# Columns by DMA transpose for half of the norm rows, a later mask fill, and a new matmul order in an attention loop

## The chip, the cores and the metric

The kernel runs on one core of one Trainium2 chip. The metric is the time of one execution on the device in microseconds (us). All numbers come from timed runs, or from profiled executions of the same kernels. The profiled span (first to last instruction) is some 1.5 to 2 us shorter than the timed execution. Engines: PE = TensorE matmul, DVE = VectorE, ACT = ScalarE, POOL = GpSimd, SP = SyncE; a "q" behind a name is that engine's instruction queue, where DMAs are issued.

A run counts as slow when it is over 1.5% above the fastest of its kernel; ratios use fast runs alone.

## The reference, cut to what matters

```python
x  = A_x                                    # 2048 rows of 512, bf16
xn = layernorm(x)
# A: attention with 32 heads of 16; row s sees rows s, s-2, ..., s-14
q, k, v = split(xn @ wqkv)
s  = softmax_over_8(q . k) . v @ wo
# B: mixer and MLP
h  = gelu(layernorm(xn) @ w1)               # then rows shifted by +-1 and +-2, @ w2
x1 = xn + shifted(h) @ w2
B  = x1 + gelu(layernorm(x1) @ w3) @ w4
out = x + s * silu(B)
```

Row s sees only rows of its own parity, so the kernel splits the rows by parity: p = 0 (chunks 0 and 1, 512 rows each) and p = 1 (chunks 2 and 3). "Second parity" means chunks 2 and 3. The attention is done in 18 units, nine per parity, of about 120 queries. It adds mask values to the scores by extra rows in the operands kT (keys) and qT (queries). Those rows are made once, written to a small memory buffer `mask_d`, and spread from there into kT and qT by DMA ("mask fill").

## The kernel before

Rows must become columns (features on partitions) before a matmul. The kernel before does that on PE: 16 transposes per chunk, a copy out by DVE, and for the second layernorm (a factor r2 per row) one more matmul that spreads r2 and a multiplication.

```python
def transposes(c, h):                        # half a chunk
    for j in range(2):
        for dt in range(ND):
            nc.tensor.transpose(pt[:, dt, j, :], x_c[:, 2*h + j, dt*P:(dt+1)*P], ident)
    nc.vector.tensor_copy(out=xnT[p][:, :, ...], in_=pt)
# rr_spread: diag(r2) by DVE -> one 128x512 matmul -> ACT copy; rr_mult: xn2T = xnT * that
...
for c in range(1, NCH):
    if c + 1 < NCH: ln_stats(c + 1)
    stage_tr(c)                              # PE transposes of chunk c
    stage_w1(c - 1)                          # first layer of B
    rr_spread(c); rr_mult(c)
    if c + 1 < NCH:
        ln_norm(c + 1); stage_qk(c)          # queries and keys
    if c == 2: fill_mask(0, 0); fill_mask(0, 1)
    if c == 1: build_mask()
stage_b(0)                                   # w2, x1, its norm; columns by DMA transpose
stage_w1(3); stage_b(1); stage_qk(3); stage_b(2)
stage_w3(0); stage_b(3); stage_w3(1); stage_w3(2); stage_w3(3)
...
# attention loop, unit n; w4 matmuls (and wo matmuls from n = 10) are spread in as filling
prs = [scores(p, u, 0)]
for f in fill[n][0]: f()                     # 8 of 11 w4 matmuls of a tile (n < 10)
prs.append(scores(p, u, 1))
for f in fill[n][1]: f()                     # the other 3
if prev is not None: weighted(*prev)         # prob @ values of the unit before, and its copy out
va = values(next unit)
```

(`...` marks cuts.) `stage_b` already has the pattern that the change uses more widely: write normed rows to memory with a plain DMA, read them back with a DMA transpose, both on the sync queue.

The softmax here doesn't subtract the row's maximum and nothing guards it: scores larger than these inputs give would overflow.

## Time and profile before

| | before |
|---|---|
| time, median of the four runs of the first comparison | 213.30 us (212.88 to 213.85) |
| profiled span | 211.9 us |
| PE busy | 201.7 us |
| granted TensorE clock | 0.999 |

From the page of the kernel before: busy us of each engine (share of the span) and number of instructions; then, below the cut, the shares of the chain of waits that ended last.

```profile
PE 201.7 (95%) x1978; PEld 96.5 (46%) x2007; DVE 131.0 (62%) x254; ACT 139.6 (66%) x160; POOL 55.5 (26%) x118
...
PE 80%; DVE 7%; DMA 5%; ACT 2%; issue 2%; POOL 1%; SPq 1%; DVEq 0%; ACTq 0%
```

PE is busy nearly always, and the chain runs over PE.

The timeline of PE, before, in the stretch that the change rebuilds. Columns: start, length, engine, source line, operation, output and inputs, shapes, count.

```profile
28.35 1.06 PE L321 MATMUL tr_ps<-ident,xn_96 128*128 128x128 bf16 x16
29.24 3.62 PE L391 MATMUL w_ps<-xn2T,w_sb 128*128 128x512 bf16 x15
32.70 0.39 PE L348 MATMUL rrep_ps<-xn2T,ones_bf 128*128 128x512 bf16 x1
32.93 7.07 PE L372 MATMUL qk_ps<-xnT_150,wqk_sb 128*128 128x512 bf16 x32
39.83 1.06 PE L321 MATMUL tr_ps<-ident,xn_96 128*128 128x128 bf16 x16
40.73 3.62 PE L391 MATMUL w_ps<-xn2T,w_sb 128*128 128x512 bf16 x15
44.18 0.38 PE L348 MATMUL rrep_ps<-xn2T,ones_bf 128*128 128x512 bf16 x1
```

No idle time stands in brackets behind any line: PE goes from one stage to the next. The transposes of a chunk (start 28.35 to next start 29.24) cost 0.89 us, the spreading matmul 0.23.

The timeline of the sync queue, before: the existing round trip through memory in `stage_b`.

```profile
55.02 0.40 SPq L436 DMA_DIRECT2D x1n_dram<-xn_662  x1
57.97 2.09 SPq L441 DMA_TRANSPOSE x1nT<-x1n_dram  x1
```

A write of 512 KB lets its transpose issue 2.95 us later. The issue of the transpose takes 2.1 us.

One unit of the attention loop, before, from the chain in order of time (start, length, what). `s_ps` are scores, `w_ps` w4, `o_ps` weighted values, `v_ps` values of the next unit.

```profile
132.45 0.34 PE s_ps L537 x16
132.79 1.83 PE w_ps L480 x8
134.63 0.51 PE s_ps L537 x16
135.14 0.76 PE w_ps L480 x3
135.89 0.53 PE o_ps L565 x32
136.43 0.32 PE v_ps L516
...
137.40 0.34 PE s_ps L537 x16
```

A unit takes 137.40 - 132.45 = 4.95 us. Sixteen full matmuls of 512 columns take 3.45 us (40.73 to 44.18 above; one record is missing there), 0.216 us each, so eight of them are 1.73 us, and the group takes 1.83.

### The profile page before, as it was taken

The page shows a single profiled execution, that of the slowest core. Times are in us where ns is not written, and L with a number is a line of the kernel's source. Part 1 is how long each engine was busy: PE and PEld are TensorE (multiplying, and loading weights), DVE is VectorE, ACT ScalarE, POOL GpSimd, SP SyncE. Part 2 cuts the span into 40 slices and gives each one's busy share as a digit, 9 for nine tenths or more (in the row PEclk, how much of TensorE's full clock was granted, in tenths as well). Part 3 has the DMA queues.
Part 4 walks back from the last instruction along what each step waited for, and adds up shares of the span by engine and source line. Part 5 has one row for each costly group of instructions (what it writes and reads, how often), then busy time and mean ns, then how long its engine had stood idle before and what let it go on. Part 6 is the DMA issues. An engine that isn't in the chain of part 4 may idle for free.

```text
span 211.9 us, 4839 instructions
## 1 busy us (share of the span) xinstructions
PE 201.7 (95%) x1978; PEld 96.5 (46%) x2007; DVE 131.0 (62%) x254; ACT 139.6 (66%) x160; POOL 55.5 (26%) x118
## 2 busy tenths in 40 slices
PE   8998999999999999999989999999999999998991
PEld 2544454544444444444444444444445544454440
DVE  6879396338839456000014666767767889688785
ACT  2098797943393625565599888788597888975310
POOL 4645774001120202000000008508039070253000
PEclk9999999999999999999999999999999999999999
DMA  5999314998240275599930003724325542445142
GB/s 152 375 395 389 117 8 6 147 145 108 99 99 3 99 198 99 140 174 126 120 39 3 0 3 61 216 80 76 114 82 141 168 103 33 129 121 107 31 147 99
DMA packets 30990, 25.16 MB, mean 119 GB/s; under 512 B 15960, under 2 KB 26424, under 8 KB 30968
## 3 DMA queue, kind: packets, MB, share of 16 engines
q1 hardware_dynamic: 27224, 19.02, 40.0%
q0 software_dynamic: 2192, 4.57, 9.1%
q10 hardware_dynamic: 1552, 1.27, 2.0%
q8 instruction: 16, 0.26, 0.6%
q14 instruction: 6, 0.05, 0.1%
HBM read 16.15 MB, written 4.37 MB: 97 GB/s over the span
## 4 chain that ended last, share of the span: by engine, by line
PE 80%; DVE 7%; DMA 5%; ACT 2%; issue 2%; POOL 1%; SPq 1%; DVEq 0%; ACTq 0%
PE w_ps L458 18%; PE w_ps L480 16%; PE qk_ps L372 10%; PE v_ps L516 7%; PE s_ps L537 7%; PE w_ps L421 6%; PE wo_ps L677 6%; PE w_ps L391 5%; PE o_ps L565 4%; DMA xn_95<-in_A_x_dram 3%; DMA oT_2427<-orw 2%; ACT prob L544 2%; DVE l1s_243 L284 1%; DVE l1s_299 L284 1%; DVE sg L686 1%
## 5 line engine op out<-in xcount | busy, mean ns | idle before, releaser
L544 ACT ACTIVATE prob<-s_ps 128x960 bf16<-128x960 f32 (+2 forms) x72 | 62.7, 925 | 11.6 <-PE s_ps L537 11.2
L480 PE MATMUL w_ps<-w_sb,h3T 128*128 128x512 bf16 (+1 forms) x174 | 43.6, 381 | 0.2 <-issue 0.2
L458 PE MATMUL w_ps<-x1nT,w_sb 128*128 128x512 bf16 (+1 forms) x173 | 38.2, 379 | 0.2
L464 ACT ACTIVATE h3T<-w_ps 128x1024 bf16<-128x1024 f32 x20 | 20.5, 1024 | 20.9 <-PE w_ps L458 20.9
L599 POOL DMA_DIRECT2D oT_1480<-orw x24 | 12.4, 525 | 61.3 <-DVE orw L572 61.3
L458 PEld LDWEIGHTS <-w_sb 128*128 128x128 bf16 (+1 forms) x176 | 17.6, 100 | 20.4
L480 PEld LDWEIGHTS <-h3T 128*128 128x128 bf16 (+1 forms) x176 | 14.7, 98 | 16.4
L521 DVE CAST v_aug_145<-v_ps 128x512 bf16<-128x512 f32 (+1 forms) x9 | 6.1, 681 | 23.1 <-PE v_ps L516 23.0
L572 DVE CAST orw<-o_ps 128x960 bf16<-128x960 f32 (+2 forms) x18 | 19.7, 1097 | 0.4 <-PE o_ps L565 0.4
L372 PEld LDWEIGHTS <-wqk_sb 128*128 128x128 bf16 x136 | 13.3, 98 | 14.3 <-issue 0.3
L599 POOL DMA_DIRECT2D oT_2427<-orw x20 | 10.1, 513 | 20.9 <-DVE orw L572 20.9
L487 DVE TENSOR_TENSOR xn_95<-w_ps,xn_95 128x512 bf16<-128x512 f32 x8 | 5.5, 692 | 16.0 <-PE w_ps L480 16.0
L372 PE MATMUL qk_ps<-xnT_149,wqk_sb 128*128 128x512 bf16 (+1 forms) x71 | 14.3, 355 | 0.3 <-DVE xnT_149 L324 0.2
L391 PE MATMUL w_ps<-xn2T,w_sb 128*128 128x512 bf16 x61 | 14.3, 379 | 0.2
L372 PE MATMUL qk_ps<-xnT_150,wqk_sb 128*128 128x512 bf16 x64 | 14.1, 379 | 0.0
L262 POOL TENSOR_SCALAR l3r<-l3m 128x4 f32<-128x4 f32 x4 | 1.0, 246 | 43.4 <-DVE l3m L270 43.4
L380 ACT ACTIVATE qT_155<-qk_ps 128x1024 bf16<-128x1024 f32 x4 | 4.1, 1030 | 9.8 <-PE qk_ps L372 9.8
L427 DVE TENSOR_TENSOR xn_96<-w_ps,xn_96 128x1024 bf16<-128x1024 f32 x4 | 4.9, 1216 | 8.3 <-PE w_ps L421 8.3
L421 PE MATMUL w_ps<-w_sb,hT_160 128*128 128x512 bf16 x32 | 9.5, 379 | 0.0
L516 PE MATMUL v_ps<-wv_sb,xnT_150 128*128 128x512 bf16 (+1 forms) x28 | 8.9, 383 | 0.4
L391 PEld LDWEIGHTS <-w_sb 128*128 128x128 bf16 x64 | 6.1, 98 | 6.8
L421 PE MATMUL w_ps<-w_sb,hT_159 128*128 128x512 bf16 x30 | 9.1, 379 | 0.1
(161 smaller groups left out, 328.8 us busy)
## 6 DMA issues: line engine op xcount, KB each, us to landing
w_sb<-in_B_w_dram SPq DMA_DIRECT2D x1, 1376.0 KB
w_sb<-in_B_w_dram SPq DMA_DIRECT2D x1, 1280.0 KB
wqk_sb<-in_A_wqkv_dram SPq DMA_DIRECT2D x2, 512.0 KB
w_sb<-in_B_w_dram SPq DMA_DIRECT2D x2, 512.0 KB
xn_96<-in_A_x_dram SPq DMA_DIRECT2D x4, 256.0 KB
xo_1598<-in_A_x_dram POOLq DMA_DIRECT2D x4, 256.0 KB, 3.9
xo_2228<-in_A_x_dram POOLq DMA_DIRECT2D x4, 256.0 KB, 3.7
out_dram<-xo_1598 SPq DMA_DIRECT2D x3, 256.0 KB
```

The costliest lines, as they stand in the source:

```text
L372: nc.tensor.matmul(pt[:, b, h : h + n], lhsT=wqk_sb[:, dt, nt * P : (nt + 1) * P], rhs=xnT[p][:, dt, k * CH + h : k * CH + h + n], start=( ...
L391: nc.tensor.matmul(pt[:, b, :], lhsT=w1_sb[:, dt, g * P : (g + 1) * P], rhs=xn2T[:, dt, :], start=(dt == 0), stop=(dt == ND - 1),)
L421: nc.tensor.matmul(pt[:, j, :], lhsT=w2_src(p, g, m0), rhs=w2_sb[:, g, :], start=(g == 0), stop=(g == ND - 1),)
L458: nc.tensor.matmul(pt[:fs, ft % 2, :], lhsT=w3_sb[:, dt, ft * P : ft * P + fs], rhs=x1nT[:, dt, :], start=(dt == 0), stop=(dt == ND - 1),)
L464: last["gelu"] = nc.scalar.activation(h3T[:, 2 * a : 2 * a + 2, :], pt, AF.Gelu_apprx_tanh)
L480: nc.tensor.matmul(pt, lhsT=h3[c][:fs, ft, jj * P : (jj + 1) * P], rhs=w4_sb[:fs, ft, :], start=(ft == 0), stop=(ft == NF - 1),)
L516: nc.tensor.matmul(vp[:nk, :], lhsT=xnT[p][:, dt, k0 : k0 + nk], rhs=wv_sb[:, dt, :], start=(dt == 0), stop=(dt == ND - 1),)
L537: nc.tensor.matmul(st[:nk, b, i * nq : (i + 1) * nq], lhsT=kT[p][e][r : r + 32, dt, k0 : k0 + nk], rhs=qT[p][e][r : r + 32, dt, q0 : q0 + ...
L544: nc.scalar.activation(prv[:nk, 2 * h : 2 * h + 2], st[:nk, :, 0 : 4 * nq], AF.Exp, scale=SCALE)
L572: pin(nc.vector.tensor_copy(out=orw[p][:, :, :, q0 - ra : q0 - ra + nq], in_=op[:, :, 0 : 4 * nq].rearrange("p j (s q) -> p j s q", q=nq),))
L599: (nc.scalar if (p, r) == (1, 2) and jj else nc.gpsimd).dma_start(out=oT[p][DH * hh : DH * (hh + 1), :, ra : ra + rw], in_=orw[p][32 * cg ...
L677: nc.tensor.matmul(pt, lhsT=oT[p][:, dt, i * P : (i + 1) * P], rhs=wo["sb"][:, dt, lo:hi], start=(dt == 0), stop=(dt == ND - 1),)
```

## The change

Its intent, in three parts:

1. Chunks 2 and 3 get their columns from memory: two writes and two DMA transposes per chunk. wv and w4 are loaded at about 60 us instead of at the start, so that these writes and transposes come ahead of all later loads.
2. The mask rows of the queries are filled behind the DMA transposes of the feed-forward stage. The mask buffer is now written by POOL, and the mask built on POOL behind chunk 2's r2.
3. In the attention loop the weighted values stand directly behind the second scores. Their copy out stays behind the filling; exponentials and tanh are pinned in order; units 10 to 13 split the w4 matmuls differently.

The diff, cut to its core:

```diff
-    wv_sb / w4_sb loads on nc.sync at the start
+    late_loads(): the same loads on nc.gpsimd, issued after last["r3"]
...
         for w in range(2):
-            pin(nc.sync.dma_start(out=mask_d[w].rearrange("r (g l) -> g r l", l=W), in_=rows[w]))
+            pin(nc.gpsimd.dma_start(out=mask_d[w].rearrange("r (g l) -> g r l", l=W), in_=rows[w]))
...
+    def dma_tr(c):
+        pin(nc.sync.dma_start(out=xn_dram[0, cs, :]..., in_=x_c))
+        for j in range(TPC):                      # xn2 = x_c * r2, four DVE operations
+            pin(nc.vector.tensor_scalar(out=xn2[:, j, :], in0=x_c[:, j, :], scalar1=r2[:, j : j + 1], ...))
+        pin(nc.sync.dma_start(out=xn_dram[1, cs, :]..., in_=xn2))
+        pin(nc.sync.dma_start_transpose(out=xnT[p][:, :, cs], in_=xn_dram[0, cs, :]))
+        pin(nc.sync.dma_start_transpose(out=xn2Ts[c], in_=xn_dram[1, cs, :]))
...
-    for c in range(1, NCH): ...
+    ln_stats(2)
+    stage_tr(1)
+    stage_w1(0)
+    rr_spread(1)
+    ln_norm(2)
+    dma_tr(2)
+    with tc.issue_after(last["r2"].ins):
+        build_mask()
+    rr_mult(1)
+    stage_qk(1)
+    ln_stats(3)
+    ln_norm(3)
+    dma_tr(3)
+    stage_w1(1)
+    stage_qk(2)
+    fill_mask(0, 0)
+    stage_w1(2)
     stage_b(0)
     stage_w1(3)
     stage_b(1)
+    with tc.issue_after(last["r3"].ins):
+        late_loads()
     stage_qk(3)
     stage_b(2)
     stage_w3(0)
     stage_b(3)
+    fill_mask(0, 1)
...
-            t, a, b, c = (n // 2 + 5, 0, 4, 5) if n % 2 == 0 else (n // 2 + 5, 5, 9, NF)
+            t, a, b, c = (n // 2 + 5, 0, 5, 5) if n % 2 == 0 else (n // 2 + 5, 5, NF, NF)
...
         prs.append(scores(p, u, 1))
+        if prev is not None:
+            op = weighted(*prev)
         for f in fill[n][1]:
             f()
         if prev is not None:
-            weighted(*prev)
+            keep(*prev[0:2], op)                  # the copy out
```

More of the change, by code (lines that the diff above doesn't have):

```diff
@@ L80 @@
     x1n_dram = dram.tile([S, D], BF16, name="x1n_dram")
+    xn_dram = dram.tile([2, M, D], BF16, name="xn_dram")
     def bigt(shape, name):
@@ L148 @@
     nc.sync.dma_start(out=w3_sb, in_=B_w3.rearrange("(dt q) f -> q dt f", q=P))
-    wv_sb = const.tile([P, ND, D], BF16, name="wv_sb")
-    nc.sync.dma_start(out=wv_sb, in_=wqkv_v[:, :, 2 * D : 3 * D])
-    w4_sb = midt([P, NF, D], "w4_sb")
-    nc.sync.dma_start(
-        out=w4_sb[:, 0 : NF - 1, :],
-        in_=B_w4[0 : (NF - 1) * P, :].rearrange("(ft q) n -> q ft n", q=P),
-    )
-    nc.sync.dma_start(out=w4_sb[0:FL, NF - 1, :], in_=B_w4[(NF - 1) * P : F, :])
     nc.scalar.preload_act_table_set("gelu_apprx_tanh_and_others")
@@ L187, in build_mask @@
         gp = nc.gpsimd
-        tab = sm4.tile([P, 3, P + 24], BF16, name="m_tab", tag="s4")
+        tab = fin.tile([P, 3, P + 24], BF16, name="m_tab", tag="f")
         for i, o, v in ((0, 0, -7), (0, 15, 8), (1, 1, -7), (1, 16, 7)):
@@ L243, in fill_mask, with late_loads @@
                 )
+    late = {}
+    def late_loads():
+        late["wv"] = const.tile([P, ND, D], BF16, name="wv_sb")
+        pin(nc.gpsimd.dma_start(out=late["wv"], in_=wqkv_v[:, :, 2 * D : 3 * D]))
+        late["w4"] = midt([P, NF, D], "w4_sb")
+        pin(
+            nc.gpsimd.dma_start(
+                out=late["w4"][:, 0 : NF - 1, :],
+                in_=B_w4[0 : (NF - 1) * P, :].rearrange("(ft q) n -> q ft n", q=P),
+            )
+        )
+        pin(nc.gpsimd.dma_start(out=late["w4"][0:FL, NF - 1, :], in_=B_w4[(NF - 1) * P : F, :]))
     NV = 2
@@ L262, in rsqrt_eps @@
         nc.gpsimd.tensor_scalar(out=dst, in0=var, scalar1=EPS, scalar2=None, op0=ALU.add)
-        nc.gpsimd.tensor_tensor(out=dst, in0=dst, in1=nhalf[:, 0 : dst.shape[-1]], op=ALU.pow)
+        return nc.gpsimd.tensor_tensor(out=dst, in0=dst, in1=nhalf[:, 0 : dst.shape[-1]], op=ALU.pow)
     def layer_stats(src, name):
@@ L271, in layer_stats @@
         rstd = small.tile([P, TPC], F32, name=name + "r", tag=name + "r")
-        rsqrt_eps(rstd, mv[:, :, 1])
+        last["r3"] = rsqrt_eps(rstd, mv[:, :, 1])
         return mv, rstd
@@ L277 @@
     lns = {}
+    last = {}
     def ln_stats(c, j0=0, n=TPC):
@@ L308, in ln_norm @@
         if j0 + n == TPC:
-            rsqrt_eps(r2, r2)
+            last["r2"] = rsqrt_eps(r2, r2)
     xn2Ts = {}
@@ L331, in stage_tr @@
             transposes(c, h)
+    def dma_tr(c):
+        p, k = c // 2, c % 2
+        cs = slice(k * CH, (k + 1) * CH)
+        x_c = xn[p][:, k * TPC : (k + 1) * TPC, :]
+        pin(nc.sync.dma_start(out=xn_dram[0, cs, :].rearrange("(i q) d -> q i d", q=P), in_=x_c))
+        r2 = r2s.pop(c)
+        xn2 = sm4.tile([P, TPC, D], BF16, name="xn2", tag="s4")
+        for j in range(TPC):
+            pin(
+                nc.vector.tensor_scalar(
+                    out=xn2[:, j, :], in0=x_c[:, j, :], scalar1=r2[:, j : j + 1], scalar2=None, op0=ALU.mult
+                )
+            )
+        pin(nc.sync.dma_start(out=xn_dram[1, cs, :].rearrange("(i q) d -> q i d", q=P), in_=xn2))
+        pin(nc.sync.dma_start_transpose(out=xnT[p][:, :, cs], in_=xn_dram[0, cs, :]))
+        xn2Ts[c] = sm4.tile([P, ND, CH], BF16, name="xn2T", tag="s4")
+        pin(nc.sync.dma_start_transpose(out=xn2Ts[c], in_=xn_dram[1, cs, :]))
     def rr_spread(c):
@@ L444 @@
     h3 = {}
-    last = {}
     def stage_w3(c):
@@ L480, in half @@
                     nc.tensor.matmul(
-                        pt, lhsT=h3[c][:fs, ft, jj * P : (jj + 1) * P], rhs=w4_sb[:fs, ft, :],
+                        pt, lhsT=h3[c][:fs, ft, jj * P : (jj + 1) * P], rhs=late["w4"][:fs, ft, :],
                         start=(ft == 0), stop=(ft == NF - 1),
@@ L491, in half @@
                     st["sig"] = fin.tile([P, D], BF16, name="sig", tag="f")
-                    nc.scalar.activation(st["sig"], x_i, AF.Tanh, scale=0.5)
+                    pin(nc.scalar.activation(st["sig"], x_i, AF.Tanh, scale=0.5))
         def gate():
@@ L516, in values @@
                 nc.tensor.matmul(
-                    vp[:nk, :], lhsT=xnT[p][:, dt, k0 : k0 + nk], rhs=wv_sb[:, dt, :],
+                    vp[:nk, :], lhsT=xnT[p][:, dt, k0 : k0 + nk], rhs=late["wv"][:, dt, :],
                     start=(dt == 0), stop=(dt == ND - 1),
@@ L543, in scores @@
             with tc.issue_after(last["gelu"].ins):
-                nc.scalar.activation(
+                pin(nc.scalar.activation(
                     prv[:nk, 2 * h : 2 * h + 2], st[:nk, :, 0 : 4 * nq], AF.Exp, scale=SCALE
-                )
+                ))
         return pr
@@ L551, in weighted @@
         r = next(i for i, x in enumerate(runs[p]) if u < x[1])
-        ra = runs[p][r][2]
         if u == runs[p][r][0]:
@@ L571, in weighted, with keep @@
                     )
+        return op
+    def keep(p, u, op):
+        q0, nq, k0, nk = units[u]
+        r = next(i for i, x in enumerate(runs[p]) if u < x[1])
+        ra = runs[p][r][2]
         pin(nc.vector.tensor_copy(
@@ L716 @@
     stage_qk(0, [1, 2, 3])
-    for c in range(1, NCH):
-        if c + 1 < NCH:
-            ln_stats(c + 1)
-        stage_tr(c)
-        stage_w1(c - 1)
-        rr_spread(c)
-        rr_mult(c)
-        if c + 1 < NCH:
-            ln_norm(c + 1)
-            stage_qk(c)
-        if c == 2:
-            fill_mask(0, 0)
-            fill_mask(0, 1)
-        if c == 1:
-            build_mask()
+    ln_stats(2)
[15 more added lines that the diff above has]
+    stage_w1(2)
     stage_b(0)
@@ L758 @@
         fill[n][0].append(lambda t=t, a=a, b=b: w4s[t][0](a, b))
+        if b == NF and n < 14:
+            fill[n + 1][0].append(w4s[t][1])
         if c > b:
@@ L803 @@
     )
-    weighted(*prev, tag="s")
+    keep(*prev[0:2], weighted(*prev, tag="s"))
     final_tile(1, 0, tag="b")
```

## The prediction

> **What bounds it now.** TensorE. The profile's busy table has PE at 201.7 of 211.9 us; the stretch table shows 9.9 to 10.0 us in nearly every 10 us from 30 to 110, and 9.84 to 9.89 from 120 to 180. The chain of waits is 80% PE. PE's idle time is about 10 us: the start (1.05 us, then warm-up), 0.67 us at 21 us (weights waiting for the diagonal from DVE), 0.52 us at the first exponentials, and the tail after 188 us. The granted clock is 0.999. So only PE time removed, or tail waits removed, can show.
>
> **What the change does.**
> 1. Chunks 2 and 3 lose their PE transposes (0.89 us of chain each: 16 matmuls) and the matmul that spreads r2 (0.22 us each): 2 x 1.11 = 2.2 us of PE, all on the chain. DVE loses two copies (1.25 us a chunk) and one multiplication (1.23), and gains four scalings (1.38); ACT loses a 0.6 us copy. None of those bound.
> 2. Added instead, per chunk: two 512 KB writes and two DMA transposes on the sync queue. The existing round trip of x1n shows the cost: write issued 55.02, transpose issued 57.97, its issue 2.1 us, data moving to about 62: some 7 us; with a second transpose about 9. My schedule: chunk 2's norm is written from about 22.5 us (the order of the DVE timeline), its transposes issue at 25.4 and 27.5, columns land at about 29.6 to 31.7. PE wants them for queries and keys at about 31.8 (two 3.45/6.9 us stages after 21.4) and the scaled ones at 38.7. The margin is 0 to 2 us. Chunk 3 must land by about 45.6; I get 42 to 45, the later if the two mask writes (2048 pieces of 16 bytes each), now issued by POOL, delay its rstd.
> 3. The DMA engines were full until 22.9 us (7.3 MB of loads). Moving wv and w4 (1.9 MB) to about 60 us frees them at about 18 us, so the new writes meet an idle queue. The moved loads fill idle DMA time.
> 4. Mask rows for queries go to about 88 us; they need about 7 us (before: 16 transfers in 40 to 52 us at 145 GB/s) and are wanted at 104. Free.
> 5. Attention loop: weighted values directly behind scores. The Trainium skill, "TensorEngine Tiling (Array Packing)", Key Properties, says that changing tiling mode drains TensorE. The trace agrees: eight w4 matmuls between two score groups take 1.83 us, against 8 x 0.216, so a return to tiles costs about 0.1 us; after the score group the cost is the same whatever follows. One such switch goes in 13 of 18 units: 1.3 us. Now that exponentials and tanh are pinned in order, tanh may come 0.05 to 0.1 us ahead of a ready exponential, and the score groups already wait some 0.15 us for exponentials: I count 0.9 us.
>
> Sum: 2.2 + 0.9 = 3.1 us, less an expected 0.3 us of new waits.
>
> **Predicted: 210.8 us, 208.6 to 214.0. Faster by over 2%: 0.18; within 2%: 0.74; slower: 0.08.**
>
> **What would show it.** No PE idle before the queries-and-keys matmuls of chunk 2 (else step 2 fails); the feed-forward stage starts about 2.2 us sooner than 65.1; the loop's period falls from 4.94 to about 4.87 us; the tail after the last scores is unchanged at about 22 us.
>
> **What would make it wrong.** DVE waiting for POOL's mask table ahead of the scaling, so that chunk 2's transposes come late and PE idles 1 to 4 us; POOL writing descriptors for the masks so long that chunk 3 stalls its first-layer matmuls; the late loads slowing x1n's second transpose, which landed only about 1 us ahead of its use; ACT, not PE, setting the loop's period.

## The result, and the profile after

The changed kernel took 218.32 us (median of four runs, 218.03 to 218.90) against 213.30. A ratio here is the mean time of one kernel's fast runs over that of the other's of the same rounds, so not quite the ratio of the medians: 1.0237, 95% interval 1.0202 to 1.0273. It is slower, and outside my range.

The same lines of the page, after:

```profile
PE 199.6 (92%) x1944; PEld 95.2 (44%) x1973; DVE 127.3 (59%) x248; ACT 138.3 (64%) x158; POOL 60.3 (28%) x123
...
PE 55%; DMA 15%; POOL 7%; DVE 7%; ACT 7%; SPq 4%; issue 3%; DVEq 0%; ACTq 0%
```

PE's busy time did fall, by 2.1 us (by 3.9, to 197.8, in a1 below, where no matmul runs at half clock), but the chain has left PE for DMA, POOL and the sync queue. The timeline of PE, after, shows where:

```profile
29.08 3.62 PE L419 MATMUL w_ps<-xn2T,w_sb 128*128 128x512 bf16 x15
32.53 7.07 PE L400 MATMUL qk_ps<-xnT,wqk_sb 128*128 128x512 bf16 x32
39.44 3.62 PE L419 MATMUL w_ps<-xn2T,w_sb 128*128 128x512 bf16 x15
42.89 3.62 PE L449 MATMUL w_ps<-w_sb,hT 128*128 128x512 bf16 x16
50.79 5.93 PE L419 MATMUL w_ps<-xn2T,w_sb 128*128 128x512 bf16 x16 [4.28 <-DMA xn2T<-xn_dram]
56.55 3.62 PE L449 MATMUL w_ps<-w_sb,hT 128*128 128x512 bf16 x16
```

The transposes and spreading matmuls of chunks 2 and 3 are gone, and chunk 2's columns came in time (no idle before 32.53). But chunk 3's first layer (50.79) waited 4.28 us for its scaled columns, and then took 50.79 to 56.55 = 5.76 us where the same stage takes 3.45 elsewhere. Stretches of the same trace, after (length, then busy us of PE, weight load, DVE, ACT and POOL, then granted clock, DMA share and GB/s; the DMA share adds up the times of packets and can pass 1), say why:

```profile
48.00:49.00 1.00, 0.00 (x0) 0.00 (x0) 1.00 (x2) 0.00 (x0) 0.00 (x0) 0.83 1.22 204
50.00:51.00 1.00, 0.21 (x1) 0.13 (x2) 0.03 (x1) 0.00 (x0) 0.80 (x2) 0.50 1.22 145
55.00:56.00 1.00, 1.00 (x5) 0.45 (x4) 0.00 (x0) 0.44 (x1) 0.00 (x0) 0.76 1.04 105
```

The granted clock fell to half during the idle time, and stayed there until 55 to 56 us. The Trainium skill, "TensorE: Matmul & The Clock Gate", What's actually happening, describes this: an idle window halves the clock until PE has been busy for a window again. The trace agrees as to the half clock and the return, which came about 5 us after the restart; the fall came only about 2 us after the last matmul (46.5 to between 48 and 49), sooner than the idle window of that page (last section).

What held chunk 3 back is read from the timelines of POOL and of the sync queue, after. First POOL:

```profile
31.23 2.58 POOL L226 DMA_DIRECT2D mask_d<-m_rows  x2
33.89 0.24 POOL L270 TENSOR_SCALAR l1r<-l1m 128x4 f32<-128x4 f32 x1
```

Then the sync queue:

```profile
36.70 0.37 SPq L347 DMA_DIRECT2D xn_dram<-xn  x1
38.45 0.37 SPq L356 DMA_DIRECT2D xn_dram<-xn  x1
42.56 3.22 SPq L357 DMA_TRANSPOSE xnT<-xn_dram  x1
45.95 2.03 SPq L359 DMA_TRANSPOSE xn2T<-xn_dram  x1
```

POOL computes chunk 3's 1/sigma (`l1r`) only after it has built the mask and spent 2.58 us on issuing the two mask writes, although DVE had the variance ready at 30.7. (DVE too was held up by the mask: it waited 0.67 us for POOL's table and began chunk 3's statistics at 28.00, against 26.38 in a1 below.) And the write issued at 36.70 released its transpose only at 42.56: 5.86 us, against 2.95 for the same size in the kernel before.

The attention loop, after, in the chain:

```profile
137.40 0.34 PE s_ps L564 x16
137.74 1.83 PE w_ps L507 x8
139.58 0.51 PE s_ps L564 x16
140.09 0.53 PE o_ps L591 x32
...
140.78 0.60 PE w_ps L507 x2
141.38 0.87 PE v_ps L543 x4
142.24 0.34 PE s_ps L564 x16
```

A unit now takes 142.24 - 137.40 = 4.84 us, 0.11 less. But in units 10 to 13, where the new split leaves nothing between the second scores and the values, this turns up on PE's timeline, after:

```profile
168.92 0.60 PE L591 MATMUL o_ps<-prob,v_aug 128*32 128x120 bf16 x32
169.46 1.04 PE L543 MATMUL v_ps<-wv_sb,xnT 128*128 128x512 bf16 x3
170.43 0.38 PE L564 MATMUL s_ps<-qT,kT 32*128 32x120 bf16 x8
171.01 0.38 PE L564 MATMUL s_ps<-qT,kT 32*128 32x120 bf16 x8 [0.20 <-ACT prob L571]
```

The second half of the first scores has to wait until ACT has read its bank.

The phases below are starts read from PE's timelines: the front runs from chunk 1's spreading matmul to the first w3 matmul, units count from their first scores, and "14 to end" closes at PE's last matmul. (The w3 stage is 42.4 us in both kernels.)

| us | front | units 0 to 9 | units 10 to 13 | 14 to end of PE |
|---|---|---|---|---|
| before | 43.90 | 49.20 | 18.43 | 32.21 |
| after | 48.42 | 48.47 | 18.93 | 32.05 |

The front lost 4.52 us, which is -2.23 for the work taken off, and 6.75 for the wait (4.28, and some 0.15 until the pipeline had drained) and the half clock (5.76 - 3.45 = 2.31). The rest won 0.73 + 0.16 and lost 0.50. The spans differ by 5.2 us. Of that, 0.74 lies ahead of these phases and 0.33 behind PE's end: chunk 1's spreading matmul stood at 21.95 instead of 21.21. Kernels with the changed kernel's code up to there had it anywhere from 21.3 to 22.0, and this profiled run (218.90) was the slowest of its four.

### The profile page after: what moved, and what is told of

Its sections match the earlier page's. It is cut to its first block, busy times and chain, and to the rows that moved or that the text cites. A ratio compares the mean times of both kernels' runs of the same rounds, so it can differ in the third digit from the quotient of the medians.

```text
span 217.1 us, 4787 instructions
## 1 busy us (share of the span) xinstructions
PE 199.6 (92%) x1944; PEld 95.2 (44%) x1973; DVE 127.3 (59%) x248; ACT 138.3 (64%) x158; POOL 60.3 (28%) x123
## 3 DMA queue, kind: packets, MB, share of 16 engines
q1 hardware_dynamic: 31592, 21.21, 45.7%
## 4 chain that ended last, share of the span: by engine, by line
PE 55%; DMA 15%; POOL 7%; DVE 7%; ACT 7%; SPq 4%; issue 3%; DVEq 0%; ACTq 0%
PE w_ps L507 17%; PE w_ps L485 10%; ACT prob L571 6%; PE s_ps L564 6%; PE wo_ps L709 5%; PE w_ps L449 5%; PE v_ps L543 4%; DMA kT<-mask_d 4%; DMA qT<-mask_d 3%; PE qk_ps L400 3%; DMA xn<-in_A_x_dram 3%; PE w_ps L419 3%; DMA xn_dram<-xn 3%; DVE l1s L293 2%; PE o_ps L591 2%
## 5 line engine op out<-in xcount | busy, mean ns | idle before, releaser
L631 POOL DMA_DIRECT2D oT<-orw x44 | 22.4, 516 | 83.5 <-issue 45.7
L507 PE MATMUL w_ps<-w_sb,h3T 128*128 128x512 bf16 (+1 forms) x164 | 40.9, 380 | 1.7 <-issue 1.6
L400 PE MATMUL qk_ps<-xnT,wqk_sb 128*128 128x512 bf16 (+1 forms) x134 | 28.4, 366 | 0.3 <-DVE xnT L333 0.2
L548 DVE CAST v_aug<-v_ps 128x512 bf16<-128x512 f32 (+1 forms) x18 | 12.3, 681 | 23.2 <-PE v_ps L543 23.2
L408 ACT ACTIVATE qT<-qk_ps 128x1024 bf16<-128x1024 f32 x16 | 15.2, 1031 | 14.7 <-PE qk_ps L400 14.7
L564 PE MATMUL s_ps<-qT,kT 32*128 32x120 bf16 (+2 forms) x576 | 18.8, 211 | 1.9 <-ACT prob L571 1.2
L564 PEld LDWEIGHTS <-kT 32*128 32x128 bf16 (+1 forms) x576 | 11.7, 94 | 18.5 <-issue 18.4
L543 PE MATMUL v_ps<-wv_sb,xnT 128*128 128x512 bf16 (+1 forms) x66 | 18.3, 380 | 0.3
L709 PE MATMUL wo_ps<-wo_sb,oT 128*128 128x512 bf16 (+1 forms) x66 | 15.5, 366 | 0.3 <-issue 0.2
L408 ACT ACTIVATE kT<-qk_ps 128x1024 bf16<-128x1024 f32 x16 | 15.2, 1082 | 0.0
L449 PE MATMUL w_ps<-w_sb,hT 128*128 128x512 bf16 x63 | 14.4, 379 | 0.1
```

The source lines that it names most:

```text
L400: nc.tensor.matmul(pt[:, b, h : h + n], lhsT=wqk_sb[:, dt, nt * P : (nt + 1) * P], rhs=xnT[p][:, dt, k * CH + h : k * CH + h + n], start=( ...
L408: nc.scalar.activation(dst[e][:, n0 : n0 + 2, k * CH : (k + 1) * CH], pt, AF.Copy)
L449: nc.tensor.matmul(pt[:, j, :], lhsT=w2_src(p, g, m0), rhs=w2_sb[:, g, :], start=(g == 0), stop=(g == ND - 1),)
L507: nc.tensor.matmul(pt, lhsT=h3[c][:fs, ft, jj * P : (jj + 1) * P], rhs=late["w4"][:fs, ft, :], start=(ft == 0), stop=(ft == NF - 1),)
L543: nc.tensor.matmul(vp[:nk, :], lhsT=xnT[p][:, dt, k0 : k0 + nk], rhs=late["wv"][:, dt, :], start=(dt == 0), stop=(dt == ND - 1),)
L564: nc.tensor.matmul(st[:nk, b, i * nq : (i + 1) * nq], lhsT=kT[p][e][r : r + 32, dt, k0 : k0 + nk], rhs=qT[p][e][r : r + 32, dt, q0 : q0 + ...
```

## The experiments

Twelve kernels ran, in three batches; all results are correct. "Before" was timed again in each batch: 213.42, 213.37 and 213.40 us.

### a1: the mask built behind chunk 3

```diff
     dma_tr(2)
-    with tc.issue_after(last["r2"].ins):
-        build_mask()
...
     dma_tr(3)
+    with tc.issue_after(last["r2"].ins):
+        build_mask()
```

> Edit: the mask table is built, and written out, after the norms and transposes of chunk 3 instead of before them; nothing else. Theory M (the mask work queued ahead of chunk 3's norm on POOL and on the DMA engines makes its columns late): POOL does chunk 3's rstd at about 30 us instead of 33.9, the write of xn takes about 3 us instead of 5.9, the scaled columns land by about 43 us, PE does not idle before the first-layer matmuls of chunk 3, the clock stays at full: 218.3 less 4.3 (idle) less 2.3 (half clock) = about 211.7, or up to 213 if the later mask fill now delays x1n's first transpose. Rival R (two writes and two serial transposes through memory are too long in themselves): PE still idles 3 us or more there and the time stays at 216 or more.

Measured: 211.98 us (211.79 to 212.39), ratio to before 0.9934 (0.9910 to 0.9957). POOL does chunk 3's 1/sigma at 29.21; the write goes out at 32.01, and its transpose at 34.83, 2.8 us later. PE has no idle time before chunk 3's first layer, the clock is 1.0, and the front takes 41.67 us: 2.23 less than before, the whole of what came off PE. (The timed medians differ by less, 1.44 us; in this profile chunk 1's spreading matmul again stood late, at 22.04.) Theory M holds and rival R falls. Two writes and two transposes per chunk are short enough; the mask work ahead of them was the trouble.

### a2 and a3: which part of the mask work

a2 keeps the mask's arithmetic where the change has it, and moves only its two writes behind chunk 3's transposes, on the sync queue. a3 leaves the writes in their place but lets the sync queue issue them.

```diff
 # a2
-            pin(nc.gpsimd.dma_start(out=mask_d[w]..., in_=rows[w]))      # in build_mask
...
     dma_tr(3)
+    write_mask()                                                         # the same two writes on nc.sync
 # a3
-            pin(nc.gpsimd.dma_start(out=mask_d[w]..., in_=rows[w]))
+            pin(nc.sync.dma_start(out=mask_d[w]..., in_=rows[w]))
```

> Edit: the mask table is computed where the change has it, but its two writes go on the sync queue behind chunk 3's transposes. Theory M, with the writes (not the arithmetic) as the culprit: POOL reaches chunk 3's rstd at about 31.3 us, 2.6 us sooner, and the write of xn meets free DMA engines: no idle before chunk 3's first layer, 211.7 to 213. If the arithmetic on POOL were the culprit, 1 us or less would be won. Rival R: no change, 218.

> Edit: the two mask writes stay in their place but are issued by the sync queue, not by POOL. It keeps the 4096 pieces of 16 bytes on the DMA engines just ahead of chunk 3's writes and takes only the 2.6 us of issuing off POOL. If POOL's time is what counts: idle falls from 4.3 to about 1.5 us. If the pieces on the DMA engines count as much: the write of xn still takes 5 us or more and idle stays at 1 to 3 us. Under both, between the change and a2: about 213 to 216.5. Rival R: 218.

The two run alike until 30 us. The sync queue of a2 from there, without the line of the second write:

```profile
33.79 0.37 SPq L352 DMA_DIRECT2D xn_dram<-xn  x1
36.60 1.93 SPq L362 DMA_TRANSPOSE xnT<-xn_dram  x1
```

And of a3, which issued the mask writes at 30.2 to 32.2 us, cut in the same way:

```profile
33.63 0.38 SPq L347 DMA_DIRECT2D xn_dram<-xn  x1
41.75 1.91 SPq L357 DMA_TRANSPOSE xnT<-xn_dram  x1
```

Without the mask writes ahead of it, the write takes 2.8 us to release its transpose; with them, 8.1. The two mask writes are only 64 KB together, but in 4096 pieces of 16 bytes. The Trainium skill, "DMA: Bandwidth & Descriptors", Specifications, says that transfers need pieces of 512 bytes or more for line rate, and that smaller ones are read, modified and written. The trace agrees in kind: in the changed kernel, from 33 to 34 us, the DMA engines were busy for 0.72 of the time and moved 22 GB/s. No run shows the reading and modifying itself, and none wrote the same 64 KB in larger pieces.

Chunk 3's write stayed slow after the packets of the pieces had gone by. In the changed kernel the last data packets of the mask writes are in the trace by 36 us, ahead of chunk 3's write (36.70); but the second mask write, issued at 32.6, landed only 8.3 us later, at about 40.9, and until then chunk 3's write was slow. Stretches, after:

```profile
39.00:40.00 1.00, 1.00 (x6) 0.49 (x5) 0.00 (x0) 1.00 (x3) 0.00 (x0) 1.00 0.92 78
41.00:42.00 1.00, 1.00 (x6) 0.44 (x5) 0.00 (x0) 1.00 (x2) 0.00 (x0) 1.00 1.04 343
```

The engines moved 78 GB/s from 39 to 40 us and 343 from 41 to 42 (a2's same write: 388 from 35 to 36). What is still busy with the pieces by then, the traces don't show.

a3 took 217.19 us (216.58 to 217.55). PE's wait fell only from 4.28 to 3.88 us, although chunk 3's write was issued 3.1 us sooner than in the changed kernel: POOL's time for issuing was won, and most of it lost to the pieces, which now stood closer in front of the write and in the same queue. That missed what I expected (1 to 3 us of wait, 213 to 216.5 us). So the pieces are enough for a wait of 3.9 us with nothing of POOL's issuing left. What POOL's 2.58 us would cost without the pieces, no run shows. An estimate from a2: its last transpose packets are in the trace before 43 us and PE came to them at 45.93, so a write 2.6 us later would have been in time, or nearly so.

a2 has no wait at chunk 3 any more, as expected, and yet took 224.05 us; its fast runs alone were 221.21 and 223.16, ratio 1.0409. I had expected 211.7 to 213. The wait of PE in its profile (a run that counts as slow, at 224.9; its fast runs too are 8 to 10 us longer than the kernel before):

```profile
PE w_ps L490 <- DMA x1nT<-x1n_dram: 11.3, 1, 11.3
```

Line by line: engine, what waited, for what; us in total, times, longest. The loss had moved to the next DMA transpose, x1n's first. Its write stood behind the late mask fill and released it only 7.55 us after its issue (52.50 to 60.05). In the meantime POOL had issued the late loads of wv and w4 (58.98 to 61.5), and the transpose, issued at 60.05, let PE go at 74.69. Experiment c2 tests that.

### a4: PE kept busy in place of the wait

```diff
     stage_b(0)
+    for i in range(22): matmul of constants, 128x512, into a spare bank
     stage_w1(3)
```

> Edit: 22 matmuls on constants (4.75 us at full clock) are put in the place of PE's idle time before chunk 3's first layer. Theory C (the first-layer matmuls behind the stall ran at half clock because PE had idled over 4 us): they take 3.6 us instead of 5.9, granted clock 1.0 throughout, time about 216 to 216.5. Rival (they ran slowly for another reason, such as the DMA traffic beside them): no gain, 218.3 to 218.8.

Measured: 216.64 us (216.26 to 216.90), just above the range. The first layer of chunk 3 took 3.45 us again (50.67 to 54.12), the clock was 1.00 through 46 to 58 us, and the front took 46.42 instead of 48.42. That is the sum: 22 x 0.216 = 4.75 us of useless matmuls in place of 4.4 of waiting, and 2.31 of half clock saved. So about a third of the loss at this wait was the clock, not the wait. (In a4's profile the second transpose was issued at 43.30, not at 45.95, behind the same code: the length of the wait differs between executions, and 4.28 us is that of the profiled one.)

### b1 and b3: the attention edits alone, and the front alone

b1 is the kernel before with part 3 of the change only. b3 is a1 with part 3 taken back (the hunks shown above, in both directions).

> The kernel before with the attention edits alone (weighted values behind scores, the new w4 split of units 10 to 13, exponentials and tanh pinned). Theory S: units 1 to 9 win 0.1 us each (about 0.8), units 10 to 13 lose about 0.9 because with no w4 matmuls between the second scores and the next first scores those first scores wait for exponentials: 213.0 to 213.8, no change. Rival P (my prediction's step 5): 212.1 to 212.5.

> The kernel with the mask behind chunk 3 (a1) with all attention edits taken back, so the front of the change alone, mended. Theory S (attention edits net to nothing): 211.6 to 212.4, as a1. Rival P: 212.7 to 213.1, because 0.9 us of gain would be given up.

b1: 213.89 us (213.31 to 214.68), ratio 1.0025 (0.9998 to 1.0052): no gain. Its phases are 48.42, 18.93 and 32.06 against 49.20, 18.43 and 32.21 before: the loop's gain of 0.78 us is mostly given back in units 10 to 13. The profiled end came 0.4 us sooner, and the timed runs don't show even that. b3: four fast runs, 211.33 to 212.25, as a1 on another chip; phases 49.19 and 18.44, those of before. Rival P falls: part 3 as a whole is worth nothing that the time shows. Its order of matmuls and its pinning were never run apart, so which of them makes the loop's gain is argued (one switch of tiling mode less), not shown. Two of b3's six runs were slow (219.13 and 219.39); see c1 and c4.

### b2 and b4: other splits of the w4 matmuls

```diff
 # b2 = a1 with
-            t, a, b, c = (n // 2 + 5, 0, 5, 5) if n % 2 == 0 else (n // 2 + 5, 5, NF, NF)
+            t, a, b, c = (n // 2 + 5, 0, 4, 5) if n % 2 == 0 else (n // 2 + 5, 5, 9, NF)
 # b4 = b2, and
+        if 14 <= n < 17:
+            b = a                    # all three w4 matmuls behind the weighted values
```

> a1 with only the w4 split of units 10 to 13 taken back (4+1 and 4+2 matmuls around the second scores instead of 5+0 and 6+0); weighted values stay behind scores. Theory S: the wait of the first scores of units 11 to 14 for exponentials (about 0.5 us each) goes, 0.7 to 1.0 us is won, 211.0 to 211.3. Rival (the loss in these units is from pinning tanh ahead of exponentials): no gain, 212.

> b2, and in units 14 to 16 the three w4 matmuls moved from ahead of the second scores to behind them and the weighted values. If in units 10 to 16 the loop is set by exponentials of the second scores, then the first scores behind them, then the matmuls ahead of the next second scores (1.84 + 0.4 + 1.6 + 0.4 = 4.3 us), each of three units falls from 4.30 to about 4.0: 0.6 to 1.0 us below b2, 210.1 to 210.6. If VectorE or PE alone set that loop: as b2.

b2: units 10 to 13 take 18.45 us again (a1: 18.93) and units 0 to 9 keep 48.48. The wait for exponentials was indeed made by the split, but it was worth 0.5 us in all, not 0.7 to 1.0. The time, 212.51 us (fast runs 211.44 to 213.11, one slow run at 219.47), doesn't show it: the profiled run waited 1.4 us for x1n's first transpose in the front (43.22 us instead of 41.67).

b4 missed: 212.99 us, and units 14 to 16 went from 13.06 to 14.87 us. PE's longest wait, in the list of waits of b4:

```profile
PE wo_ps L709 <- DVE v_aug L548: 2.3, 4, 1.2
```

The wo matmuls share their bank with the values, which DVE copies out behind the w4 addition and the weighted values' copy. Where I had freed PE from ACT, it ran into DVE's order. The third possibility of my text, "as b2", was not right either.

### c1, c2 and c4: the loads back at the start

c1 is a1, c2 is a2 and c4 is b2, each with wv and w4 loaded at the start on the sync queue, as the kernel before does.

```diff
+    late["wv"], late["w4"] loaded on nc.sync behind w3, before the norms
...
-    with tc.issue_after(last["r3"].ins):
-        late_loads()
```

> a1 with wv and w4 loaded at the start on the sync queue, as the kernel before does, instead of at 59 us. Theory L (moving the loads was not needed for chunk 2's columns: the loads end near 22.9 us and the first write of xn goes out at 23.3; at 59 us they share the DMA engines with x1n's first transpose): no new idle in front of chunk 2's queries and keys, 211.5 to 212.2, and no run 2% above the others. Rival (the loads had to go for the columns to come in time): idle of 1 us or more before chunk 2's queries and keys, 213 or more.

> a2 (mask writes behind chunk 3's transposes on the sync queue; 224 us, PE idle 11.3 us for x1n's first transpose, which took 14 us to land) with the same loads back at the start. Theory L: the transpose, issued at about 60, lands about 4 us after its issue, idle before the feed-forward stage falls from 11.3 to 1 or 2 us, 212.5 to 214.5. Rival (the mask fill in front of it on the sync queue is the whole delay): idle stays above 8 us, 221 or more.

> b2 (mask behind chunk 3, old w4 split of units 10 to 13) with the loads back at the start: the version that I expect to be best. Phases of b2 without its 1.5 us stall at the feed-forward stage: 211.0 to 211.6, no slow run; below the kernel before and the changed kernel in every round.

c1: 211.66 us (211.45 to 211.87), the front 41.66, no idle before chunk 2's queries and keys. The first write of chunk 2 goes out at 22.57, while the loads end; its transpose issues at 26.14, 3.6 us later (a1: 23.30 and 26.10, 2.8 us). Beside the end of the loads that write took 0.8 us longer, which the margin covers: moving them was not needed for the columns.

c2: 212.86 us (212.41 to 213.68). PE's wait for x1n's first transpose falls from 11.3 to 1.7 us. That transpose was issued at 60.25, as late as in a2 (60.05), and with an unchanged mask fill in front of it. The late loads made the difference: about 14.6 us from its issue to PE's start beside them, 4.6 us without them (60.25 to the first w3 matmul at 64.81). The Trainium skill, "DMA: Bandwidth & Descriptors", Queues, rings and completion order, says that each DMA engine takes turns between the queues at packet granularity. The trace fits such sharing, though it doesn't show the turns themselves: from 64 to 68 us, a2's sync queue, with the transpose, had 22.5% of the engines' time, and the queue of the loads 90.5%.

c4: 211.06 us (210.70 to 211.16), ratio 0.9889 (0.9874 to 0.9903). This is the best version, 1.1% faster than the kernel before: phases 41.67, 48.47, 18.45 and 32.05. No run of c1 or c4 was slow, where b2 and b3, with the late loads, had three slow runs of twelve at 219 us; the ten runs of a1 and b4, with the late loads too, had none. It fits that those runs lost the race with the loads; they were not profiled, so that is argued, not shown.

### c3: the mask rows of the queries filled early

```diff
     fill_mask(0, 0)
+    fill_mask(0, 1)
...
     stage_b(3)
-    fill_mask(0, 1)
```

> a1 with the mask rows for queries filled directly behind those for keys, as before, instead of behind the feed-forward's transposes. If that part of the change is needed: 1 MB more (about 8 us at the 125 GB/s that such fills ran at) stands ahead of x1n's first write, its transpose comes 6 to 8 us later, PE idles 4 to 8 us before the feed-forward stage and half clock follows: 217 to 222. If it is not: as a1, 212.

Measured: 221.90 us (220.99 to 222.65), ratio 1.0398. From the list of PE's waits in c3:

```profile
PE w_ps L485 <- DMA x1nT<-x1n_dram: 6.8, 1, 6.8
```

x1n's first write goes out at 56.56 (a1: 53.03) and its transpose at 63.32 (a1: 56.50). So this part of the change is needed in the new order: with the fill of the queries' rows in its old place, the front would lose 7 us. (The late loads, at 60 us, stand beside that transpose too, so not all of the 7 us is the fill. An estimate without them: issued at 63.32, and with the 4.6 us that such a transpose took in c2, it lets PE go at 67.9, where PE had ended its work at 63.2.)

## Why the prediction was wrong, point by point

- **What bounds it: right.** PE did, and in the profiles of a1 and c4 the front is shorter by all of the 2.23 us that came off PE. The timed medians gained 1.44 us in a1, and 2.34 in c4 with the loop's gain in it.
- **Step 1 (PE time removed): right.** I said 2.2 us; the front of a1, b3 and c4 is 2.23 us shorter.
- **Step 2, chunk 2: right.** Its columns were there without a wait. **Step 2, chunk 3: this is the step that failed.** "Chunk 3 must land by about 45.6; I get 42 to 45, the later if the two mask writes ... delay its rstd." PE could start on the scaled columns only at 50.79. Its write went out 4.7 us later than in a1 (36.70 against 32.01) and took 3.0 us longer (5.86 against 2.8). I had costed the mask writes as POOL's time, which was there (2.58 us), but not what they do to the DMA behind them. They added 5.3 us to the write right behind them (a3 against a2: 8.1 against 2.8 us), and 2.9 us of that showed in the changed kernel (5.86 against 2.95). I took the length of that write from a place in the trace where no such pieces ran in front of it. The same trace had shown the pieces: from 31 to 34 us the mask writes of the kernel before kept the DMA engines busy for 0.88 of the time, at 17 GB/s.
- **The size of the loss was missing.** I listed a chunk 3 stall by the mask under "what would make it wrong", but as POOL "writing descriptors", and allowed nothing for the half clock. A wait of 4.28 us cost 6.75 us, 2.31 of them at the clock (a4).
- **Step 3 (moved loads fill idle DMA time): half right.** They did no harm in the changed kernel's profile, where x1n's first transpose came ahead of them. But the move was not needed (c1), and it is a trap: a2 lost 11.3 us to it.
- **Step 4 (queries' mask rows late is free): right, and more.** In the new order it is needed (c3).
- **Step 5 (loop): the mechanism fits, its sum was wrong.** A unit fell from 4.95 to 4.84 us (I said 4.94 to 4.87). The term that failed is "13 of 18 units": units 10 to 13, whose split the change alters, lost 0.50 us in place of a gain, because the first scores behind a bare second-scores, weighted-values and values sequence wait for ACT (b2 takes the loss away).

Together: I had 3.1 us of gain less 0.3 of waits. The runs show 2.2 in the front and at most 0.4 in the loop, less 6.75 at one wait. With that wait and the new split gone, the four phases of c4 are together 3.1 us shorter than before, the gain that I had summed; its timed median is 2.34 us shorter.

## What to carry to other kernels

When work moves from an engine to DMA, cost what goes ahead of it on the DMA engines, and look at the pieces, not only the bytes: 64 KB in pieces of 16 bytes held up a 512 KB write by 5 us. Look at every later transfer of the same queue too, since a fill or a load moved out of one deadline's way lands in front of the next (a2, c3). And a wait of PE can bring the half clock with it: here all four waits from 3.9 to 11.3 us did (a3, the changed kernel, c3, a2; a further 2.3 us in the changed kernel), while the clock stayed at 1.0 through those of 1.4 and 1.7 us (b2, c2).

## What the Trainium skill lacked or had wrong

- "DMA: Bandwidth & Descriptors", Anatomy of one DMA: its fit of 2.0 us plus bytes / 436e3 gives an estimate of about 2.1 us for a 32 KB write issued by GpSimd. The mask writes of 32 KB in 16-byte pieces landed after 5.8 to 8.3 us, and each took POOL 1.2 to 1.4 us to issue. The fit lacks a term for the number of pieces; what the page says elsewhere of small descriptors doesn't enter it. No page has that a later write stays slow until such pieces have landed (78 against 343 GB/s).
- The same page, Rules for kernel authors, says that a transpose next to ordinary DMAs needs nothing. That is about correct data; it gives no cost. Beside 1.9 MB of loads a transpose of 512 by 512 let PE go only about 14.6 us after its issue, against 4.6 us without them (a2, c2).
- The same page has bandwidths for the DMA transpose, and a count of sequencer cycles for small tiles, but not what a large one costs its issuing queue. Here, on the sync queue, 512 by 512 in bf16 took 1.3 to 2.7 us of issue in most cases, and up to 4.6 (c3).
- "TensorE: Matmul & The Clock Gate", What's actually happening: it names an idle window of about 3.4 us. In the changed kernel the clock fell some 2.2 us after the last matmul had ended; in a3, c3 and a2 it fell 4.3, 5.0 and 5.2 us after it (worked out from the mean clock of the one stretch of 1 us in which it fell). The page does say that the window runs freely, which may be why the delays differ; but 2.2 us is less than one whole idle window. No wait between 1.7 and 3.9 us was profiled, so whether a shorter one already costs the clock stays open.
